# Four one-bank accumulators for the down product, and an earlier request of batch 1's first two row pairs, in a Fourier mix followed by a gated feed-forward network

## The chip, the core and the metric

One core of a Trainium2 chip runs the whole program. The time is device microseconds of one launch; the number that counts is the median of several runs. Inside the profile, times are counted in microseconds from the first instruction of the span. The engines are PE (matrix multiplications, with PEld for its weight loads), DVE, ACT and POOL (elementwise work) and SP, which here only issues DMA transfers.

## The reference

Two stages follow each other. The first is a Fourier mix over 8 sequences (called batches below) of 3008 tokens with 256 features:

```python
X = np.fft.rfft(x, axis=1)
Yr = Xr @ w_r - Xi @ w_i + b_r
Yi = Xr @ w_i + Xi @ w_r + b_i
Yr = np.sign(Yr) * np.maximum(np.abs(Yr) - lam, 0.0)
Yi = np.sign(Yi) * np.maximum(np.abs(Yi) - lam, 0.0)
y = np.fft.irfft(Yr + 1j * Yi, n=x.shape[1], axis=1)
```

The second is a feed-forward network over the 24064 tokens that come out, with 2048 hidden features:

```python
h = x @ w_in
g = h * (1.0 / (1.0 + np.exp(-1.702 * h)))
out = (g @ w_out).astype(np.float32)
```

## The kernel before, in words

**The Fourier part.** `spectral(b, s2)` makes the steps of one batch. Stage A (16 steps, `split_x` and `stage_a`, lines 261 to 288) loads a slice of the input (`xa` or `xr`), multiplies it by a constant matrix (line 283 in plain 32 bits for batches 0 to 2, `mm3` for the others), copies the bank on ACT to `aev` and stores that to a scratch tensor `s1` in DRAM. Stage B (12 steps, `stage_b`) reads back a pair of rows `br` of `s1` with its constants `kr` (`load_b`) and multiplies them (line 312). `load_b(0)` needs all 16 stores of its batch. `stage_b(0)` requests pairs 0 and 1, and each later step requests one pair ahead. `stage_mix` multiplies by the weights, `stage_inv` transforms back and stores `iev` to a scratch tensor `s2`. `tokens` reads `s2` as `ur`, transforms once more (line 408) and splits the tokens of a feed-forward tile into `th` and `tl`.

**The feed-forward part.** Its 47 tiles have 512 tokens each; a tile has eight quarters of the hidden features, q = 0 to 7. `up(q)` makes two banks of 128 by 512 with six matmuls of `mm3` each: a 32-bit product is three products of rounded halves (lines 130, 131 and 132: high by high, high by low, low by high). ACT applies the activation into `gb` (line 440) and rounds it to `hb`; DVE makes the remainder `lb`; sums of them give `gt`, split into `ht` (ACT) and `lt` (DVE), line 127. `down(q)` multiplies them by the weights in the order of the table `ORDER`, seven products of three matmuls of 128 by 256, and adds them up in the accumulator `po` over all eight quarters. The accumulator is one tile of four banks (8 KB in each partition), `self.acc[:, bk, h]`, with one buffer.

**The end of a tile.** After q = 7, `combine` (lines 499 to 511) reads the accumulator: ACT copies bank 0 (line 502), six DVE operations read the banks in the order 1, 2, 3, 1, 1, 2 (lines 503, 504, 505, 506, 508 and 509), POOL adds one pair (line 507), SP stores two outputs. Line 505 is the last reader of bank 3, line 508 that of bank 1, line 509 that of bank 2. The last tile of all has its own `combine_last` (lines 483 to 497), and its last two quarters multiply plain 32-bit values (line 477).

**The order of the work.** A loop over 47 x 8 quarters calls `up(q)`, then `fill(3)`, which takes six entries (three stage A steps) off a list `filler` with stage A of batches 1 and 2, then steps of a queue of later spectral work in proportion to their costs, then `tokens_to`, then `down` of the quarter before. A scheduler reorders each engine's instructions when the program is built: by the dependences between tiles, by a timing model of its own, and by when buffers come free. It follows a tile as a whole: a buffer is free for its next tile when every reader of the old tile is done. The pool `ps_o` holds the accumulator (four banks), the pool `ps_a` four banks `pa` for everything else. Tiles of 128 by 512 (`xr`, `aev`, `br`, `mv`, `yr`, `iev`, `ur`, `o0`, `o1`, `uv` and others) share seven places (`buf2`).

**The start.** `hold_clock` issues a few spare matmuls into a `po` tile while PE would wait.

Of the kernel before, what the change touches and what calls it, by code (L numbers as in the profile page):

```python
# [9 lines left out]
F32 = mybir.dt.float32  # L10
# [5 lines left out]
ALU = mybir.AluOpType  # L16
# [10 lines left out]
TOK, HT = 512, 256  # L27
# [78 lines left out]
def fourier_mix_then_gated_ffn(ctx: ExitStack, tc: tile.TileContext, x, w_r, w_i, b_r, b_i, w_in, w_out, pack, kbs, out):  # L106
    nc = tc.nc
# [6 lines left out]
    ps_o = ctx.enter_context(tc.tile_pool(name="ps_o", bufs=1, space=PSUM))  # L114
    ps_a = ctx.enter_context(tc.tile_pool(name="ps_a", bufs=4, space=PSUM))

    def bank():
        return ps_a.tile([128, 512], F32, name="pa", tag="pa")

    def buf(shape, dt, name, tag=None, bufs=2):  # L120
        return wk.tile(shape, dt, name=name, tag=tag or name, bufs=bufs)

    def buf2(name):
        return buf([128, 2, D], F32, name, tag="w2", bufs=W2)

    def split(hi, lo, src):
        return nc.scalar.copy(hi, src).ins, nc.vector.tensor_tensor(lo, src, hi.bitcast(F32), ALU.subtract).ins  # L127

    def mm3(ps, wh, wl, xh, xl, start=True, stop=True):
        nc.tensor.matmul(ps, lhsT=wh, rhs=xh, start=start, stop=False)  # L130
        nc.tensor.matmul(ps, lhsT=wh, rhs=xl, start=False, stop=False)  # L131
        nc.tensor.matmul(ps, lhsT=wl, rhs=xh, start=False, stop=stop)  # L132
# [38 lines left out]
    wo_h = cst.tile([128, NQ, 7, 128], F32R, name="wo_h")  # L171
    wo_l = cst.tile([128, NQ, 7, 128], F32R, name="wo_l")
# [69 lines left out]
    def spectral(b, s2):  # L242
# [4 lines left out]
        xs, raw, zs, ys = {}, {}, {}, {}  # L247
# [42 lines left out]
        def load_b(sp):  # L290
            if plain:
                kt = buf([128, 3, D], F32, "br0", tag=("zh", "zl")[sp % 2])
                t, k = kt[:, 0:2], kt[:, 2].rearrange("p (i n) -> p i n", i=2)
            else:
                t, k = buf2("br"), buf([128, 2, 2 * N1], F32, "kr")
            with tc.issue_after(stored[13]):
                nc.sync.dma_start(k, kbs[sp])
            nc.sync.dma_start(t, s1r[2 * sp:2 * sp + 2].rearrange("s p d -> p s d"))
            raw[sp] = t, k

        def stage_b(sp):

            ahead = 3 if plain else 1
            for n in range(0 if sp == 0 else sp + ahead, min(sp + ahead + 1, 12)):
                load_b(n)
            t, k = raw.pop(sp)
            co = buf([128, 2, 3, 128], F32, "co")
            pv = bank().rearrange("p (c v i n) -> p c v i n", c=2, v=2, i=2)
            for i in range(2):
                for c in range(2):  # L310
                    cs = slice(128 * c, 128 * c + 128)
                    nc.tensor.matmul(pv[:, c, :, i], lhsT=t[:, i, cs], rhs=k[:, i], start=True, stop=True)  # L312
            nc.scalar.copy(co[:, :, 0:2], pv.rearrange("p c v i n -> p c v (i n)"))
            nc.vector.tensor_tensor(co[:, :, 2], co[:, :, 0], co[:, :, 1], ALU.add)
            z = co.rearrange("p c v n -> p (c v) n")
            if plain:
                zs[sp] = z
                return
            zh = buf([128, 6, 128], F32R, "zh")
            zl = buf([128, 6, 128], F32R, "zl")  # L320
            split(zh, zl, z)
            zs[sp] = zh, zl
# [56 lines left out]
        first, second = [], []  # L379
# [6 lines left out]
            for n in range(4):  # L386
                load_x(n)

        return first, second, preload


    s2s, us, ytiles = {}, {}, {}
# [32 lines left out]
    class Ffn:  # L425
# [43 lines left out]

        def down(self, q):  # L470
            if q == 0:
                self.acc = ps_o.tile([128, 4, 2, HT], F32, name="po", tag="po")
            g = self.g.pop(q)
            for n, (a, t, bk, h) in enumerate(ORDER):
                start, stop = q == 0 and FIRST[bk] == n, q == NQ - 1 and LAST[bk] == n
                if not isinstance(g[t], tuple):
                    nc.tensor.matmul(self.acc[:, bk, h], lhsT=self.w32[q][:, a], rhs=g[t], start=start, stop=stop)
                else:
                    mm3(self.acc[:, bk, h], wo_h[:, q, a], wo_l[:, q, a], *g[t], start=start, stop=stop)
            if q == NQ - 1:  # L480
                (self.combine_last if self.k == NT - 1 else self.combine)()

        def combine_last(self):

            p = self.acc
            o0, o1, uv = buf2("o0"), buf2("o1"), buf2("uv")
            v = nc.vector
            nc.scalar.copy(o0, p[:, 0])
            v.tensor_tensor(uv[:, 0], p[:, 1, 0], o0[:, 0], ALU.add)
            nc.gpsimd.tensor_tensor(o0[:, 0], o0[:, 0], o0[:, 1], ALU.add)  # L490
            v.tensor_tensor(o0[:, 1], uv[:, 0], p[:, 1, 1], ALU.add)
            v.tensor_tensor(uv[:, 1], p[:, 2, 0], uv[:, 0], ALU.add)
            v.tensor_tensor(o0[:, 1], o0[:, 1], p[:, 2, 1], ALU.add)
            nc.sync.dma_start(out[self.k, :, 0], o0.rearrange("p h n -> p (h n)"))
            v.tensor_tensor(o1[:, 1], uv[:, 1], p[:, 1, 1], ALU.add)
            v.tensor_tensor(o1[:, 0], uv[:, 1], p[:, 3, 0], ALU.subtract)
            nc.scalar.dma_start(out[self.k, :, 1], o1.rearrange("p h n -> p (h n)"))

        def combine(self):
            p = self.acc  # L500
            o0, o1, uv = buf2("o0"), buf2("o1"), buf2("uv")
            nc.scalar.copy(o0, p[:, 0])
            nc.vector.tensor_tensor(uv[:, 0], p[:, 1, 0], o0[:, 0], ALU.add)
            nc.vector.tensor_tensor(uv[:, 1], p[:, 2, 0], uv[:, 0], ALU.add)
            nc.vector.tensor_tensor(o1[:, 0], uv[:, 1], p[:, 3, 0], ALU.subtract)
            nc.vector.tensor_tensor(o1[:, 1], uv[:, 1], p[:, 1, 1], ALU.add)
            nc.gpsimd.tensor_tensor(o0[:, 0], o0[:, 0], o0[:, 1], ALU.add)
            nc.vector.tensor_tensor(o0[:, 1], uv[:, 0], p[:, 1, 1], ALU.add)
            nc.vector.tensor_tensor(o0[:, 1], o0[:, 1], p[:, 2, 1], ALU.add)  # L509
            for e, o in enumerate((o0, o1)):  # L510
                nc.sync.dma_start(out[self.k, :, e], o.rearrange("p h n -> p (h n)"))

    def hold_clock(ins, count):

        with tc.issue_after(ins):
            o = ps_o.tile([128, 4, 2, HT], F32, name="po", tag="po").rearrange("p c h n -> p (c h n)")
            for _ in range(count):
                nc.tensor.matmul(o[:96, 0:446], lhsT=ka32, rhs=kc[:96, 0:446], start=True, stop=True)

# [2 lines left out]
    def new_s2(b):  # L522
        s2s[b] = dr.tile([48, 2, NJ, D], F32, name="s2")
        return s2s[b]

    assert NB > 2
    (first, second, _), (first1, queue, preload), (first2, queue2, _) = (spectral(b, new_s2(b)) for b in range(3))
    nextb = 2
    for n, (_, step) in enumerate(first + second):
        step()  # L530
# [8 lines left out]
    filler = first1 + first2  # L539
    last_aev = evacuated[15]  # L540

    def fill(count):
        for _ in range(2 * count):
            if filler:
                filler.pop(0)[1]()

    def weights(q):
        with ExitStack() as held:

            for ins in ([last_aev] if q < 5 else mixed if q == 5 else first_tokens) if q else ():  # L550
                held.enter_context(tc.issue_after(ins))
            up_weights(q, q > 5)
            down_weights(q, q > 5)
# [24 lines left out]
    for n in range(NT * NQ):  # L578
        k, q = divmod(n, NQ)
        if n in (1, 3):  # L580
            weights(6 + n // 2)
        if q == 0:
            cur = Ffn(k)
        cur.up(q)
        fill(3)
        if not queue and nextb < NB:
            if nextb == 2:
                queue = queue2
            else:
                first, second, _ = spectral(nextb, new_s2(nextb))  # L590
                queue = first + [(4000, lambda: None)] + second
            nextb += 1
            total = None
        if queue and total is None and not filler:
            total, spent, n0 = sum(c for c, _ in queue), 0.0, n
            n1 = NQ * S * (nextb - 1) // TOK - 12
        while queue and total and spent < total * (n + 1 - n0) / (n1 - n0):
            c, step = queue.pop(0)
            spent += c
            step()  # L600
        need = TOK * (1 + (n + 2) / NQ)
        while queue and need + JP > S * (nextb - 1):
            queue.pop(0)[1]()
        if JP * done < need:
            tokens_to(need)
        if behind is not None:
            behind[0].down(behind[1])
        behind = (cur, q)
# [37 lines left out]
```

## Time and profile before

| | us |
|---|---|
| median of 3 runs | 2633.46 (2631.92 to 2638.31) |
| the profiled execution | 2632.74 |
| its span, first to last instruction | 2630.6 |
| PE busy in the span | 2589.7 (98%) |
| DVE, ACT, POOL busy | 1967.4, 1642.7, 53.8 |

The page of the profile gives busy times and the clock that PE was granted. The view of waits sums, by pair of instructions, how long an engine stood idle for another. The view by windows gives each engine's busy time and the mean granted clock in stretches of the span. The timeline lists instructions with their start, their length and, in brackets, the idle time before them with what ended it. Matmuls are pipelined, so the distance from one start to the next is what a matmul takes of PE's time; its length is more.

### The profile page before, as it was taken

What the parts mean: (1) busy time and instruction counts of PE and PEld (TensorE: products, weight loads), DVE (VectorE), ACT (ScalarE), POOL (GpSimd) and SP (SyncE); (2) the same over time, 40 slices, a digit from 0 to 9 for tenths busy, and PEclk for the clock granted to TensorE, in tenths of its full rate; (3) what the DMA queues carried; (4) which work ended last, traced back from release to release, by engine and by line L of the source; (5) the groups of instructions that cost most, each with busy time, mean ns of one, the idle gap of its engine ahead of it and who ended that gap; (6) DMA issues with size and microseconds to landing.
All of it is one profiled execution on the core that took longest, in us unless ns stands there. A gap on an engine that the chain in (4) does not pass through costs nothing.

```text
span 2630.6 us, 42804 instructions
## 1 busy us (share of the span) xinstructions
PE 2589.7 (98%) x16520; PEld 2327.6 (88%) x16520; DVE 1967.4 (75%) x3219; ACT 1642.7 (62%) x2547; POOL 53.8 (2%) x71
## 2 busy tenths in 40 slices
PE   7899999999999999999999999999999999999998
PEld 4679999999899998999989999899998999999998
DVE  6767877777777777777777777778777777777676
ACT  5566666666666666666676666766667666655554
POOL 1000000000000000000000000000000000000000
PEclk8899999999999999999999999999999999999999
DMA  8652221111322223212241221322213122200000
GB/s 259 205 171 71 82 86 49 50 59 55 95 79 62 69 62 103 74 60 68 64 124 56 68 67 60 120 63 61 75 60 121 47 74 62 66 18 32 18 20 17
DMA packets 156075, 200.64 MB, mean 76 GB/s; under 512 B 18688, under 2 KB 105600, under 8 KB 155872
## 3 DMA queue, kind: packets, MB, share of 16 engines
q1 hardware_dynamic: 153360, 189.26, 23.7%
q0 software_dynamic: 2368, 8.39, 1.0%
q8 instruction: 130, 2.13, 0.4%
q14 instruction: 73, 0.60, 0.1%
q10 hardware_dynamic: 144, 0.26, 0.0%
HBM read 97.70 MB, written 74.97 MB: 66 GB/s over the span
## 4 chain that ended last, share of the span: by engine, by line
PE 90%; issue 7%; DMA 2%; DVE 1%; ACT 1%; POOL 0%; SPq 0%; POOLq 0%; DVEq 0%; ACTq 0%
PE pa L130 16%; PE pa L131 16%; PE pa L132 16%; PE po L130 11%; PE po L131 11%; PE po L132 11%; PE pa L408 4%; PE pa L312 3%; PE pa L283 1%; PE pa L331 1%; DMA wraw<-in_w_in 1%; DMA s<-aev 0%; PE pa L366 0%; DMA yr<-mv 0%; ACT gb L440 0%
## 5 line engine op out<-in xcount | busy, mean ns | idle before, releaser
L440 ACT ACTIVATE gb<-pa 128x512 f32<-128x512 f32 x752 | 447.0, 598 | 424.0 <-PE pa L132 421.4
L127 DVE TENSOR_TENSOR lt<-gt,ht 128x1024 fp32r<-128x1024 f32 x374 | 458.3, 1226 | 246.8 <-ACT ht L127 245.7
L130 PE MATMUL pa<-th,wi_h 128*128 128x512 f32 x1504 | 597.5, 397 | 2.9 <-ACT gb L440 2.1
L131 PE MATMUL pa<-tl,wi_h 128*128 128x512 f32 x1504 | 591.4, 393 | 0.0
L132 PE MATMUL pa<-th,wi_l 128*128 128x512 f32 x1504 | 588.1, 391 | 0.0
L127 ACT CAST ht<-gt 128x1024 fp32r<-128x1024 f32 x374 | 391.5, 1047 | 158.5 <-DVE gt L462 146.8
L131 PE MATMUL po<-lt,wo_h 128*128 128x256 f32 x1496 | 427.0, 285 | 0.0
L130 PE MATMUL po<-ht,wo_h 128*128 128x256 f32 x1496 | 425.1, 284 | 0.0
L132 PE MATMUL po<-ht,wo_l 128*128 128x256 f32 x1496 | 423.3, 283 | 0.0
L127 DVE TENSOR_TENSOR lb<-gb,hb 128x768 fp32r<-128x768 f32 x375 | 358.7, 957 | 43.2 <-ACT hb L127 41.0
L460 DVE TENSOR_TENSOR gt<-gb 128x512 f32<-128x512 f32 x374 | 261.7, 700 | 134.5 <-ACT gb L440 131.1
L127 ACT CAST hb<-gb 128x768 fp32r<-128x768 f32 x375 | 313.4, 836 | 69.2 <-PE po L132 62.3
L132 PEld LDWEIGHTS pa<-th,wi_l 128*128 128x128 f32 x1504 | 283.5, 188 | 57.3
L130 PEld LDWEIGHTS pa<-th,wi_h 128*128 128x128 f32 x1504 | 284.9, 189 | 52.0 <-ACT gb L440 3.3
L130 PE MATMUL po<-hb,wo_h 128*128 128x256 f32 x1125 | 327.5, 291 | 0.9 <-DVE o L509 0.9
L131 PEld LDWEIGHTS pa<-tl,wi_h 128*128 128x128 f32 x1504 | 284.7, 189 | 44.4 <-DVE wa L198 0.5
L131 PE MATMUL po<-lb,wo_h 128*128 128x256 f32 x1125 | 319.9, 284 | 0.0
L132 PE MATMUL po<-hb,wo_l 128*128 128x256 f32 x1125 | 319.0, 284 | 0.0
L132 PEld LDWEIGHTS po<-ht,wo_l 128*128 128x128 f32 x1496 | 285.7, 191 | 8.6 <-issue 1.7
L131 PEld LDWEIGHTS po<-lt,wo_h 128*128 128x128 f32 x1496 | 285.6, 191 | 8.7 <-issue 1.8
L130 PEld LDWEIGHTS po<-ht,wo_h 128*128 128x128 f32 x1496 | 285.5, 191 | 3.8 <-issue 1.3
L130 PEld LDWEIGHTS po<-hb,wo_h 128*128 128x128 f32 x1125 | 214.8, 191 | 10.1 <-issue 2.6
(123 smaller groups left out, 3780.0 us busy)
## 6 DMA issues: line engine op xcount, KB each, us to landing
s<-aev SPq DMA_DIRECT2D x128, 192.0 KB, 2.6
br<-s SPq DMA_DIRECT2D x96, 256.0 KB, 3.0
yr<-mv SPq DMA_DIRECT2D x384, 64.0 KB, 2.0
s<-iev SPq DMA_DIRECT2D x96, 256.0 KB, 2.3
ur<-s SPq DMA_DIRECT2D x128, 192.0 KB, 2.8
out<-o SPq DMA_DIRECT2D x93, 256.0 KB, 2.1
xr<-in_x SPq DMA_DIRECT2D x80, 192.0 KB, 3.1
kr<-in_kbs SPq DMA_DIRECT2D x84, 128.0 KB, 2.1
```

Of the source, the lines that this page charges most:

```text
L127: return nc.scalar.copy(hi, src).ins, nc.vector.tensor_tensor(lo, src, hi.bitcast(F32), ALU.subtract).ins
L130: nc.tensor.matmul(ps, lhsT=wh, rhs=xh, start=start, stop=False)
L131: nc.tensor.matmul(ps, lhsT=wh, rhs=xl, start=False, stop=False)
L132: nc.tensor.matmul(ps, lhsT=wl, rhs=xh, start=False, stop=stop)
L283: done_a.append(nc.tensor.matmul(ps[:96], lhsT=ka32, rhs=xs.pop(q), start=True, stop=True).ins)
L312: nc.tensor.matmul(pv[:, c, :, i], lhsT=t[:, i, cs], rhs=k[:, i], start=True, stop=True)
L331: nc.tensor.matmul(ps, lhsT=z[:, 3 * c + v], rhs=wf32[v][:, c], start=c == 0, stop=c == 1)
L408: turned.append(nc.tensor.matmul(pv[:, c, 94 * j:94 * j + 94], lhsT=t[:, j, 128 * c:128 * c + 128], rhs=kz, start=True, stop=True).ins)
L440: nc.scalar.activation(o, ps.rearrange("p (h n) -> p h n", h=2), AF.Gelu_apprx_sigmoid)
L460: nc.vector.tensor_tensor(gt[:, 0:2], b12, gb[:, 0:3:2], ALU.subtract)
```

## The change

It has two parts.

The accumulator becomes four tiles of one bank, each with a name and a buffer of its own (`po0` to `po3`). The matmuls and the operations of `combine` and `combine_last` are the same and read the same data. What differs is what the scheduler may assume: each bank is free for the next tile when its own last reader is done, a reader of one bank waits for the matmuls into that bank, and matmuls into different banks are not tied to each other.

The rows of batch 1's pairs 0 and 1 are requested by a new `preload_b`, which the loop calls once after `fill(3)` when at most 12 entries of `filler` are left. These 12 are six stage A steps of batch 2; batch 1's stage A has been issued in full by then. `stage_b` leaves out requests that were made.

```diff
             for n in range(0 if sp == 0 else sp + ahead, min(sp + ahead + 1, 12)):
-                load_b(n)
+                if n not in raw:
+                    load_b(n)
...
-        return first, second, preload
+        def preload_b():
+            load_b(0)
+            load_b(1)
+
+        return first, second, preload, preload_b
...
             if q == 0:
-                self.acc = ps_o.tile([128, 4, 2, HT], F32, name="po", tag="po")
+                self.acc = [ps_o.tile([128, 2, HT], F32, name="po", tag=f"po{i}") for i in range(4)]
...
-                    mm3(self.acc[:, bk, h], wo_h[:, q, a], wo_l[:, q, a], *g[t], start=start, stop=stop)
+                    mm3(self.acc[bk][:, h], wo_h[:, q, a], wo_l[:, q, a], *g[t], start=start, stop=stop)
...
-            nc.scalar.copy(o0, p[:, 0])
-            nc.vector.tensor_tensor(uv[:, 0], p[:, 1, 0], o0[:, 0], ALU.add)
+            nc.scalar.copy(o0, p[0])
+            nc.vector.tensor_tensor(uv[:, 0], p[1][:, 0], o0[:, 0], ALU.add)
...
-            o = ps_o.tile([128, 4, 2, HT], F32, name="po", tag="po").rearrange("p c h n -> p (c h n)")
+            o = ps_o.tile([128, 2, HT], F32, name="po", tag="po0").rearrange("p h n -> p (h n)")
...
         cur.up(q)
         fill(3)
+        if preload_b and len(filler) <= 12:
+            preload_b()
+            preload_b = None
```

The built programs have the same number of instructions on PE, DVE, ACT, POOL and SP. Their order differs from about the first quarter of tile 0 on. Three places matter below. Line numbers of the changed kernel are up to eight higher than before.

SP, at the end of stage A of batch 2, before the change (`s1_87` is that batch's scratch tensor, `s1_85` that of batch 1, `aev` the stored slices, `xa` the loaded ones):

```order
L288 DMA s1_87<-aev_1537 96x512
L288 DMA s1_87<-aev_1544 96x512
L259 DMA xa_1604<-in_x 96x512
L288 DMA s1_87<-aev_1601 96x512
L288 DMA s1_87<-aev_1608 96x512
L288 DMA s1_87<-aev_1613 96x512
L288 DMA s1_87<-aev_1668 96x512
L298 DMA br_1676<-s1_85 128x2x256
L298 DMA br_1680<-s1_85 128x2x256
L288 DMA s1_87<-aev_1673 96x512
```

And with it:

```order
L288 DMA s1_87<-aev_1540 96x512
L288 DMA s1_87<-aev_1547 96x512
L298 DMA br_1550<-s1_85 128x2x256
L298 DMA br_1554<-s1_85 128x2x256
L259 DMA xa_1615<-in_x 96x512
L288 DMA s1_87<-aev_1612 96x512
L288 DMA s1_87<-aev_1619 96x512
L288 DMA s1_87<-aev_1624 96x512
L288 DMA s1_87<-aev_1679 96x512
```

The two requests of `br` stand six stores earlier, between the last two loads of `xa`.

PE, at the start of stage A of batch 4, which falls together with the end of a feed-forward tile, before the change (`pa_10737` is the second bank of an `up`, `pa_10769` that of the first stage A step):

```order
L131 MATMUL po_10182<-lt_10597,wo_h_80 128x256
L132 MATMUL po_10182<-ht_10596,wo_l_81 128x256
L131 MATMUL pa_10737<-tl_9884,wi_h_78 128x512
L132 MATMUL pa_10737<-th_9883,wi_l_79 128x512
L130 MATMUL pa_10737<-th_9883,wi_h_78 128x512
L131 MATMUL pa_10737<-tl_9884,wi_h_78 128x512
L132 MATMUL pa_10737<-th_9883,wi_l_79 128x512
L130 MATMUL pa_10769<-xh_10765,ka_73 96x512
L130 MATMUL pa_10782<-xh_10778,ka_73 96x512
L408 MATMUL pa_10791<-kc_69,ur_10542 128x94 x4
```

And with it (`po_10846` to `po_10849` are the four banks of the next tile):

```order
L132 MATMUL po_10847<-ht_10720,wo_l_81 128x256
L130 MATMUL po_10846<-hb_10793,wo_h_80 128x256
L130 MATMUL po_10848<-hb_10717,wo_h_80 128x256
L131 MATMUL po_10848<-lb_10718,wo_h_80 128x256
L132 MATMUL po_10848<-hb_10717,wo_l_81 128x256
L130 MATMUL po_10848<-ht_10720,wo_h_80 128x256
L131 MATMUL po_10848<-lt_10721,wo_h_80 128x256
L132 MATMUL po_10848<-ht_10720,wo_l_81 128x256
L130 MATMUL po_10848<-hb_10793,wo_h_80 128x256
L130 MATMUL pa_10817<-xh_10813,ka_73 96x512
L130 MATMUL pa_10830<-xh_10826,ka_73 96x512
```

The first matmul on `xh` stood directly behind the six matmuls of an `up`; now the last `up` before it ends 23 matmuls earlier, all 23 of the next tile's `down`.

PE, at the end of the program, before the change (`po_27752` is the accumulator, L477 the plain 32-bit products):

```order
L131 MATMUL po_27752<-lb_27992,wo_h_80 128x256
L132 MATMUL po_27752<-hb_27991,wo_l_81 128x256
L130 MATMUL po_27752<-hb_27991,wo_h_80 128x256
L131 MATMUL po_27752<-lb_27992,wo_h_80 128x256
L132 MATMUL po_27752<-hb_27991,wo_l_81 128x256
L477 MATMUL po_27752<-gl_27993,w32_27994 128x256 x4
L477 MATMUL po_27752<-gb_28022,w32_28040 128x256 x3
L477 MATMUL po_27752<-gl_28039,w32_28040 128x256 x4
```

And with it (`po_27890` is bank 0, then 27891, 27892 and 27893 are banks 1, 2 and 3; their plain products are on L482):

```order
L130 MATMUL po_27892<-hb_28132,wo_h_80 128x256
L131 MATMUL po_27892<-lb_28133,wo_h_80 128x256
L132 MATMUL po_27892<-hb_28132,wo_l_81 128x256
L482 MATMUL po_27891<-gl_28134,w32_28135 128x256
L482 MATMUL po_27892<-gl_28134,w32_28135 128x256
L482 MATMUL po_27892<-gb_28163,w32_28181 128x256
L482 MATMUL po_27891<-gl_28134,w32_28135 128x256
L482 MATMUL po_27891<-gl_28180,w32_28181 128x256 x2
L482 MATMUL po_27893<-gl_28134,w32_28135 128x256
L482 MATMUL po_27892<-gl_28180,w32_28181 128x256
L482 MATMUL po_27893<-gl_28180,w32_28181 128x256
```

Bank 0 has no matmul among these last ones any more, bank 1 ends three matmuls and bank 2 one matmul ahead of the last. DVE's last six operations were lines 489, 491, 492, 493, 495 and 496 in this order; in the changed program, in the numbers of before, they are 489 (bank 1), 492 (bank 2), 491 (bank 1), 495 (bank 1), 496 (bank 3) and 493 (bank 2).

More of the change, by code (lines that the diff above doesn't have):

```diff
@@ L476, in down @@
                 if not isinstance(g[t], tuple):
-                    nc.tensor.matmul(self.acc[:, bk, h], lhsT=self.w32[q][:, a], rhs=g[t], start=start, stop=stop)
+                    nc.tensor.matmul(self.acc[bk][:, h], lhsT=self.w32[q][:, a], rhs=g[t], start=start, stop=stop)
                 else:
-                    mm3(self.acc[:, bk, h], wo_h[:, q, a], wo_l[:, q, a], *g[t], start=start, stop=stop)
+                    mm3(self.acc[bk][:, h], wo_h[:, q, a], wo_l[:, q, a], *g[t], start=start, stop=stop)
             if q == NQ - 1:
@@ L487, in combine_last @@
             v = nc.vector
-            nc.scalar.copy(o0, p[:, 0])
-            v.tensor_tensor(uv[:, 0], p[:, 1, 0], o0[:, 0], ALU.add)
+            nc.scalar.copy(o0, p[0])
+            v.tensor_tensor(uv[:, 0], p[1][:, 0], o0[:, 0], ALU.add)
             nc.gpsimd.tensor_tensor(o0[:, 0], o0[:, 0], o0[:, 1], ALU.add)
-            v.tensor_tensor(o0[:, 1], uv[:, 0], p[:, 1, 1], ALU.add)
-            v.tensor_tensor(uv[:, 1], p[:, 2, 0], uv[:, 0], ALU.add)
-            v.tensor_tensor(o0[:, 1], o0[:, 1], p[:, 2, 1], ALU.add)
+            v.tensor_tensor(o0[:, 1], uv[:, 0], p[1][:, 1], ALU.add)
+            v.tensor_tensor(uv[:, 1], p[2][:, 0], uv[:, 0], ALU.add)
+            v.tensor_tensor(o0[:, 1], o0[:, 1], p[2][:, 1], ALU.add)
             nc.sync.dma_start(out[self.k, :, 0], o0.rearrange("p h n -> p (h n)"))
-            v.tensor_tensor(o1[:, 1], uv[:, 1], p[:, 1, 1], ALU.add)
-            v.tensor_tensor(o1[:, 0], uv[:, 1], p[:, 3, 0], ALU.subtract)
+            v.tensor_tensor(o1[:, 1], uv[:, 1], p[1][:, 1], ALU.add)
+            v.tensor_tensor(o1[:, 0], uv[:, 1], p[3][:, 0], ALU.subtract)
             nc.scalar.dma_start(out[self.k, :, 1], o1.rearrange("p h n -> p (h n)"))
@@ L501, in combine @@
             o0, o1, uv = buf2("o0"), buf2("o1"), buf2("uv")
-            nc.scalar.copy(o0, p[:, 0])
-            nc.vector.tensor_tensor(uv[:, 0], p[:, 1, 0], o0[:, 0], ALU.add)
-            nc.vector.tensor_tensor(uv[:, 1], p[:, 2, 0], uv[:, 0], ALU.add)
-            nc.vector.tensor_tensor(o1[:, 0], uv[:, 1], p[:, 3, 0], ALU.subtract)
-            nc.vector.tensor_tensor(o1[:, 1], uv[:, 1], p[:, 1, 1], ALU.add)
+            nc.scalar.copy(o0, p[0])
+            nc.vector.tensor_tensor(uv[:, 0], p[1][:, 0], o0[:, 0], ALU.add)
+            nc.vector.tensor_tensor(uv[:, 1], p[2][:, 0], uv[:, 0], ALU.add)
+            nc.vector.tensor_tensor(o1[:, 0], uv[:, 1], p[3][:, 0], ALU.subtract)
+            nc.vector.tensor_tensor(o1[:, 1], uv[:, 1], p[1][:, 1], ALU.add)
             nc.gpsimd.tensor_tensor(o0[:, 0], o0[:, 0], o0[:, 1], ALU.add)
-            nc.vector.tensor_tensor(o0[:, 1], uv[:, 0], p[:, 1, 1], ALU.add)
-            nc.vector.tensor_tensor(o0[:, 1], o0[:, 1], p[:, 2, 1], ALU.add)
+            nc.vector.tensor_tensor(o0[:, 1], uv[:, 0], p[1][:, 1], ALU.add)
+            nc.vector.tensor_tensor(o0[:, 1], o0[:, 1], p[2][:, 1], ALU.add)
             for e, o in enumerate((o0, o1)):
@@ L526, in fourier_mix_then_gated_ffn @@
     assert NB > 2
-    (first, second, _), (first1, queue, preload), (first2, queue2, _) = (spectral(b, new_s2(b)) for b in range(3))
+    (first, second, *_), (first1, queue, preload, preload_b), (first2, queue2, *_) = (spectral(b, new_s2(b)) for b in range(3))
     nextb = 2
@@ L589, in fourier_mix_then_gated_ffn @@
             else:
-                first, second, _ = spectral(nextb, new_s2(nextb))
+                first, second, *_ = spectral(nextb, new_s2(nextb))
                 queue = first + [(4000, lambda: None)] + second
```

## The prediction

> **What bounds the kernel now.** I read the page first, then PE's waits, then the windows around them.
>
> ```profile
> span 2630.6 us, 42804 instructions
> ...
> PE 2589.7 (98%) x16520; PEld 2327.6 (88%) x16520; DVE 1967.4 (75%) x3219; ACT 1642.7 (62%) x2547; POOL 53.8 (2%) x71
> ...
> PEclk8899999999999999999999999999999999999999
> ```
>
> PE is busy for 98% of the span, and the change leaves its matmuls as they are. So it can win only what PE loses: the 41 us in which it is idle, and stretches at a lower clock. The waits of PE that the change can reach, in the view of waits (total, times, longest), are these.
>
> ```profile
> PE pa L312 <- DMA br<-s: 2.2, 1, 2.2
> PE pa L130 <- ACT xh L127: 2.1, 1, 2.1
> PE pa L130 <- ACT gb L440: 2.1, 3, 0.7
> PE po L130 <- DVE o L509: 0.9, 1, 0.9
> PE pa L130 <- DVE mv L336: 0.9, 2, 0.5
> ```
>
> The wait that the four banks should remove, the next tile's first down matmul on line 509, costs PE 0.9 us, once in 46 tile ends. The windows place all the losses (PE's busy time comes first behind the length).
>
> ```profile
> 193.00:205.00 12.00, 9.81 (x55) 8.78 (x54) 7.49 (x14) 6.65 (x11) 0.72 (x1) 0.86 0.56 181
> 205.00:1010.00 805.00, 804.58 (x5321) 737.48 (x5321) 615.72 (x998) 512.10 (x788) 12.76 (x14) 1.00 0.22 67
> 1010.00:1025.00 15.00, 12.89 (x68) 10.75 (x67) 11.91 (x20) 9.55 (x15) 0.73 (x1) 0.89 0.35 106
> 1025.00:2600.00 1575.00, 1571.51 (x10223) 1430.89 (x10222) 1184.45 (x1896) 990.53 (x1520) 25.53 (x30) 1.00 0.21 64
> 2600.00:2631.00 31.00, 23.67 (x149) 21.31 (x147) 16.51 (x28) 9.18 (x13) 0.72 (x1) 0.96 0.05 17
> ```
>
> Between 205 and 2600 us PE idles 0.4 + 2.1 + 3.5 = 6.0 us in 2395. At 193 to 205 it idles 2.2 us, and in the last window 7.3 us. The earlier idle time lies ahead of the first instruction that the change moves on PE (at about 131 us), so I leave it.
>
> **The change part by part.** *The request of br.* PE and then SP, around the start of batch 1's stage B:
>
> ```profile
> 194.76 0.28 PE L132 MATMUL po<-ht,wo_l 128*128 128x256 f32 x1
> 197.23 2.86 PE L312 MATMUL pa<-kr,br 128*128 128x128 f32 x16 [2.19 <-DMA br<-s]
> ```
> ```profile
> 185.69 8.01 SPq L288 DMA_DIRECT2D s<-aev  x4
> 193.79 0.92 SPq L298 DMA_DIRECT2D br<-s  x2
> ```
>
> The two requests (line 298) stood behind four stores of batch 2, the last of which SP could issue only at about 193.7; the rows landed at 197.1, 3.3 us after the request. Now they stand ahead of these four stores, so they go out before 185.7 and land by 189, some 4 us ahead of need. The 2.19 us of idle PE go. The clock goes with them:
>
> ```profile
> 199.00:200.00 1.00, 1.00 (x7) 1.00 (x6) 1.00 (x3) 0.00 (x0) 0.70 (x1) 0.50 0.49 158
> ```
>
> About 1 us behind the gap the granted clock is at 0.50. The window of 12 us has a mean of 0.86, so 12 x 0.14 = 1.7 us of PE's time are lost on top, and the term is 2.2 + 1.7 = 3.9 us. [...]
>
> What the move costs: each br takes one of seven places that the next aev copies want, and SP waits at it for the landing of an earlier store, with the last load of xa and four stores queued behind. That load is made three stage A steps ahead of its use, and these steps lie about 2 us apart there (four stores, one a step, over 8.0 us in the row above), so a wait of some 2 to 3 us, like the 3.3 us that br's rows took to land, is covered by 6; without the cover they would fall on PE. I take nothing, with 3 us as the other end.
>
> *The tail.* PE's last matmuls, and all that follows them:
>
> ```profile
> 2621.78 1.89 PE L477 MATMUL po<-gl,w 128*128 128x256 f32 x8
> 2623.71 0.59 ACT L488 COPY o<-po 128x512 f32<-128x512 f32 x1 [6.55 <-PE po L477]
> 2624.33 0.43 DVE L489 TENSOR_TENSOR uv<-po,o 128x256 f32<-128x256 f32 x1 [5.52 <-ACT o L488]
> 2624.83 0.72 POOL L490 TENSOR_TENSOR o<-o 128x256 f32<-128x256 f32 x1 [35.13 <-DVE uv L489]
> 2625.59 0.42 DVE L491 TENSOR_TENSOR o<-uv,po 128x256 f32<-128x256 f32 x1 [0.83 <-POOL o L490]
> 2625.93 0.42 DVE L492 TENSOR_TENSOR uv<-po,uv 128x256 f32<-128x256 f32 x1
> 2626.92 0.41 DVE L496 TENSOR_TENSOR o<-uv,po 128x256 f32<-128x256 f32 x1
> ```
>
> ACT's copy of bank 0 waits for the very last matmul, which writes bank 3. From PE's end (2623.67) to DVE's (2627.33) it takes 3.66 us, and 3.3 us more for the last store. Now the copy, line 489 and POOL's sum run while PE still works: bank 1 ends three matmuls early, at 1.89 / 4 = 0.47 us each. Line 492 can start 0.47 us before PE's end, when bank 2 is complete. Four operations follow at 0.33 us from start to start (2625.59 to 2625.93), the last ending 0.41 us after its start: -0.47 + 0.04 + 4 x 0.33 + 0.41 = 1.3 us behind PE's end. The gain is 3.66 - 1.3 = 2.4 us at most. Against it, the order of the tail's matmuls is new: the last quarter's plain products of bank 0 now wait for the last activation with some two dozen short matmuls between, where before all other down products stood there. The bound from the other side is nothing gained; I take 1.9 us.
>
> *The new order of matmuls.* With four tiles the scheduler mixes `up` and `down` more finely; by my count of the two programs PE changes from 256-wide to 512-wide matmuls 702 times, before 575 times. The first fence has the last 256-wide matmul of a run and the start of a run of 512-wide ones, the second a pair far inside one:
>
> ```profile
> 1012.66 0.28 PE L132 MATMUL po<-hb,wo_l 128*128 128x256 f32 x1
> 1012.78 0.40 PE L130 MATMUL pa<-th,wi_h 128*128 128x512 f32 x1
> 1013.02 0.40 PE L131 MATMUL pa<-tl,wi_h 128*128 128x512 f32 x1
> ```
> ```profile
> 2608.35 0.39 PE L132 MATMUL pa<-th,wi_l 128*128 128x512 f32 x1
> 2608.57 0.39 PE L130 MATMUL pa<-th,wi_h 128*128 128x512 f32 x1
> ```
>
> From start to start the 256-wide one takes 0.12 us, the 512-wide one behind it 0.24, and the one of the second fence 0.22. So 127 more entries cost up to 127 x 0.02 = 2.5 us, or nothing if the entries are short runs; I take 1.0.
>
> *The waits in between.* The largest, at the start of batch 4 (PE, then ACT):
>
> ```profile
> 1019.22 1.00 PE L130 MATMUL pa<-xh,ka 96*96 96x512 f32 x2 [2.07 <-ACT xh L127]
> ```
> ```profile
> 1017.19 0.60 ACT L440 ACTIVATE gb<-pa 128x512 f32<-128x512 f32 x1 [0.58 <-PE pa L132]
> 1017.82 0.83 ACT L127 CAST hb<-gb 128x768 fp32r<-128x768 f32 x1
> 1018.56 0.61 ACT L127 CAST xh<-xr 96x512 fp32r<-96x512 f32 x1
> ```
>
> ACT does the activation of the `up` that PE has just ended, then hb, then xh, and PE has nothing else in its order. It idles 2.1 us, and the window's clock of 0.89 over 15 us adds 1.7: 3.8 us. In the changed order 23 matmuls of `down` stand between that `up` and xh. At 0.12 us each they last 2.8 us, more than the 2.1 that PE idles. This gap should go. It is an accident of the order, though, and a new order has accidents of its own. The other 3.9 us I leave as large as they are.
>
> What is new in kind lies at the 46 tile ends. The next tile's down matmuls may now be placed nearer to `combine`, bank by bank. The one place where they wait today (PE, then DVE):
>
> ```profile
> 2055.15 0.36 PE L130 MATMUL po<-hb,wo_h 128*128 128x256 f32 x1 [0.92 <-DVE o L509]
> ```
> ```profile
> 2053.27 0.41 DVE L505 TENSOR_TENSOR o<-uv,po 128x256 f32<-128x256 f32 x1
> 2054.60 0.41 DVE L509 TENSOR_TENSOR o<-o,po 128x256 f32<-128x256 f32 x1
> ```
>
> Bank 3 is free at line 505's end, 1.3 us before line 509 frees bank 2, so this wait shrinks or goes. But two such waits of 0.75 us elsewhere cost the 1.5 us that I put against the gap at 1017: net 3.8 - 1.5 = 2.3 us gained, with bounds from 7.7 gained (6.0 idle and 1.7 of clock all gone) to 4 lost (another gap like the one at 1017 and none removed).
>
> *The sum* against the profiled execution's 2632.74 us: - 3.9 - 1.9 + 1.0 - 2.3 = - 7.1, which gives 2625.6. The median of the runs before is 0.7 above that execution, so 2633.46 - 7.1 = 2626.4.
>
> **The rivals.** *The gaps only move (nothing net in the middle).* The new order has as many accidents as the old. Then - 3.9 - 1.9 + 1.0 = - 4.8 and 2628.7; if a gap takes the place of the one at 195 too, because L312 then waits for something else, 2632. For it: three of the five waits above are of kinds that neither part touches.
>
> *The order closes nearly all gaps.* With banks free one by one PE always finds down work: - 3.9 - 2.4 - 7.7 + 0.5 = - 13.5, or 2620.0. For it: PE idles so seldom that one good order is enough. Against: the scheduler's model sets that order, not the chip.
>
> *The tile ends begin to wait: slower.* The first matmul into each bank stands closer to the release, and DVE's queue holds other work between the lines of `combine` (line 462's sum stood between 508 and 509 at 2054 us). A mean wait of 0.35 us at 46 ends is 16 us, or five gaps like that at 1017 (3.8 us with their clock) are 19. With the 5.8 us of the first two terms gained, it decides from a mean of 0.13 us at 46 ends on, and at 0.35 us it gives 2633.46 - 5.8 + 1.0 + 16 = 2644.7. Against: of 46 ends today one waits. [...]
>
> *The request is not early.* If SP held at the br rows until the aev store has landed and stage A slipped by it, the gap at 195 would turn into one at 190: 2633.46 - 1.9 + 1.0 - 2.3 = 2630.3.
>
> **How the numbers follow.** About 0.3%, or 7.9 us, is what a measurement of this kernel can tell from no change; faster means below 2625.6, slower above 2641.4. My forecast has 0.48, spread from 2623 to 2630 by the tail (0 to 2.4) and the accidents, with a third of it under 2625.6. Gaps only moved, or an ineffective request: 0.24 together. All gaps closed: 0.22. Tile ends that wait: 0.06, nearly all of it slower. So faster 0.16 + 0.22 = 0.38, slower 0.05, the same 0.57. The range for 8 in 10 reaches from 2620 (gaps closed) to 2632 (gaps moved) and leaves out the slower case.
>
> **What would show it right or wrong.** Right: no wait of L312 (L313 in the changed file) on br near 195, and no half clock there; from PE's last matmul to DVE's last operation 1.3 us and not 3.7; no gap of 2 us at batch 4's start; idle PE between 205 and 2600 of about 4 us. Wrong: a new gap of 2 us or more with half clock behind it, waits of po matmuls on lines 505 to 509 at many tile ends, or a PE span that grows while its idle time does not.

## The result and the profile after

The changed kernel takes 2620.14 us in the median of 6 runs (2619.57 to 2622.23), before 2633.59 us (2631.92 to 2638.31, 6 runs). The ratio is 0.9947 with a 95% interval of 0.9934 to 0.9960: faster, by 13.5 us. I forecast 7.1 us as the likeliest gain and put the chance of a gain above 0.3% at 0.38; the time came out at the value of the rival in which the order closes nearly all gaps (2620.0). By its terms that is partly chance, as shown further down.

The page of the changed kernel, with the three ACT groups used further down (busy time, then mean length in ns):

```profile
span 2617.8 us, 42900 instructions
...
PE 2584.1 (99%) x16520; PEld 2323.9 (89%) x16520; DVE 1965.8 (75%) x3219; ACT 1644.3 (63%) x2547; POOL 57.4 (2%) x71
...
L445 ACT ACTIVATE gb<-pa 128x512 f32<-128x512 f32 x752 | 448.0, 597 | 457.4 <-PE pa L132 454.9
...
L127 ACT CAST ht<-gt 128x1024 fp32r<-128x1024 f32 x374 | 391.6, 1047 | 149.7 <-DVE gt L467 144.6
...
L127 ACT CAST hb<-gb 128x768 fp32r<-128x768 f32 x375 | 313.6, 836 | 33.3 <-PE po L132 25.9
```

The 96 more instructions than before are semaphore operations, by balance; the engines' work is the same in number. PE's idle time in the span fell from 2630.6 - 2589.7 = 40.9 us to 33.7. The view of waits between 190 and 2605 us, where five pairs stood before, has one left:

```profile
PE po L131 <- DVE lb L127: 1.6, 1, 1.6
```

The windows at the places of the prediction (length, then PE's busy time; the mean granted clock stands behind the five engines):

```profile
193.00:205.00 12.00, 12.00 (x88) 10.98 (x87) 10.41 (x20) 7.74 (x13) 0.73 (x1) 1.00 0.42 137
205.00:1010.00 805.00, 805.00 (x5321) 738.44 (x5320) 615.43 (x999) 513.64 (x791) 15.39 (x14) 1.00 0.22 68
1010.00:1025.00 15.00, 15.00 (x95) 13.28 (x94) 12.26 (x22) 9.91 (x17) 0.74 (x1) 1.00 0.51 155
1025.00:2600.00 1575.00, 1573.30 (x10242) 1433.66 (x10241) 1189.39 (x1900) 996.15 (x1522) 26.50 (x30) 1.00 0.21 64
```

Between 205 and 2600 us PE idles 1.7 us where it idled 6.0, and both windows with half clock, 0.86 and 0.89 before, show 1.00.

SP at the end of batch 2's stage A:

```profile
182.02 1.00 SPq L298 DMA_DIRECT2D br<-s  x2
186.40 0.34 SPq L259 DMA_DIRECT2D xa<-in_x  x1
```

The two requests leave at 182.0 us in place of 193.8, and the load of `xa` behind them follows at 186.4 (185.1 before) without a wait of PE.

The tail, PE's last matmuls and then DVE:

```profile
2609.97 2.75 PE L482 MATMUL po<-gl,w 128*128 128x256 f32 x12
```
```profile
2611.53 0.42 DVE L494 TENSOR_TENSOR uv<-po,o 128x256 f32<-128x256 f32 x1 [3.75 <-issue]
2612.33 0.42 DVE L497 TENSOR_TENSOR uv<-po,uv 128x256 f32<-128x256 f32 x1 [0.38 <-PE po L482]
2612.79 0.42 DVE L496 TENSOR_TENSOR o<-uv,po 128x256 f32<-128x256 f32 x1
2613.13 0.41 DVE L500 TENSOR_TENSOR o<-uv,po 128x256 f32<-128x256 f32 x1
2613.46 0.41 DVE L501 TENSOR_TENSOR o<-uv,po 128x256 f32<-128x256 f32 x1
2613.79 0.41 DVE L498 TENSOR_TENSOR o<-o,po 128x256 f32<-128x256 f32 x1
```

PE ends at 2612.72. Line 494 (489 before) runs 1.2 us ahead of that, line 497 (492) 0.4 us ahead, and four operations follow: DVE ends 1.5 us behind PE, before 3.7.

**What I had not looked at: where in a tile the waits lie.** Here is the place of the longest one in the kernel before once more, this time with what stands around it: the last down product of a tile on PE, the copy of bank 0, line 509, and the next tile's first down product.

```profile
1015.70 0.28 PE L132 MATMUL po<-ht,wo_l 128*128 128x256 f32 x1
...
1016.02 0.59 ACT L502 COPY o<-po 128x512 f32<-128x512 f32 x1 [0.94 <-PE po L132]
...
1020.37 0.41 DVE L509 TENSOR_TENSOR o<-o,po 128x256 f32<-128x256 f32 x1
...
1023.63 0.41 PE L130 MATMUL po<-hb,wo_h 128*128 128x256 f32 x1
```

For 7.9 us PE has no down product. Until 1020.78, the end of line 509, it can have none, because the one tile of four banks cannot be written again before; the order then puts the first one 2.9 us later still. The gap at 1017 lies inside. So do all the others: I took the 46 stretches between the last down matmul of a tile and the first of the next, from start to start. The first runs from 194.76 to 205.06 us and holds the wait on br; the other 45 are 431 of the 2395 us from 205 to 2600 (18%) and hold all 6.02 us of PE's idle time there. The same place in the changed kernel:

```profile
1008.92 0.59 ACT L507 COPY o<-po 128x512 f32<-128x512 f32 x1
...
1011.03 0.28 PE L132 MATMUL po<-ht,wo_l 128*128 128x256 f32 x1
...
1012.77 0.28 PE L130 MATMUL po<-hb,wo_h 128*128 128x256 f32 x1
...
1013.35 0.41 DVE L513 TENSOR_TENSOR o<-uv,po 128x256 f32<-128x256 f32 x1
```

Both ends have moved. ACT's copy of bank 0 starts 2.1 us before the tile's last down matmul, since bank 0 is complete earlier; and the next tile's down products begin while `combine` still has sums to do. The stretch without down products is 1.7 us long in place of 7.9.

### The profile page after: what moved, and what is told of

Read it like the earlier page. It is cut to its first block, busy times and chain, and to the rows that moved or that the text cites. A ratio compares the mean times of both kernels' runs of the same rounds, so it can differ in the third digit from the quotient of the medians.

```text
span 2617.8 us, 42900 instructions
## 1 busy us (share of the span) xinstructions
PE 2584.1 (99%) x16520; PEld 2323.9 (89%) x16520; DVE 1965.8 (75%) x3219; ACT 1644.3 (63%) x2547; POOL 57.4 (2%) x71
## 4 chain that ended last, share of the span: by engine, by line
PE 95%; DMA 2%; issue 2%; DVE 0%; ACT 0%; SPq 0%; POOL 0%; POOLq 0%; DVEq 0%; ACTq 0%
PE pa L130 17%; PE pa L131 17%; PE pa L132 17%; PE po L130 12%; PE po L131 12%; PE po L132 12%; PE pa L413 4%; PE pa L313 3%; PE pa L332 1%; PE pa L283 1%; DMA wraw<-in_w_in 1%; DMA wraw<-in_w_out 0%; DMA s<-aev 0%; DMA xa<-in_x 0%; DMA br<-s 0%
## 5 line engine op out<-in xcount | busy, mean ns | idle before, releaser
L131 PE MATMUL po<-lt,wo_h 128*128 128x256 f32 x1496 | 408.7, 286 | 0.0
L132 PE MATMUL po<-ht,wo_l 128*128 128x256 f32 x1496 | 405.3, 284 | 0.0
L127 DVE TENSOR_TENSOR lb<-gb,hb 128x768 fp32r<-128x768 f32 x375 | 360.3, 961 | 26.9 <-ACT hb L127 25.7
L130 PE MATMUL po<-ht,wo_h 128*128 128x256 f32 x1496 | 354.6, 284 | 0.1
L130 PE MATMUL po<-hb,wo_h 128*128 128x256 f32 x1125 | 320.6, 294 | 0.0
L130 PEld LDWEIGHTS po<-ht,wo_h 128*128 128x128 f32 x1496 | 259.0, 190 | 10.3 <-issue 1.8
L131 PEld LDWEIGHTS po<-lb,wo_h 128*128 128x128 f32 x1125 | 214.4, 191 | 10.8 <-DVE lb L127 1.8
```

## The experiments

Two theories stood against each other for the 4.3 us of waits that went between 205 and 2600 us. Theory 1: they are a property of the one tile, which keeps PE from any down product at each tile end. Theory 2: the order is a draw, as the prediction had it ("a new order has accidents of its own"), and this one was lucky. For each kernel I worked out from its order how much PE time stands between the down products of one tile and the next (0.12 us for a 256-wide matmul, 0.227 for a 512-wide one; 46 ends). All ratios are to the kernel before on the same chip. The labels are explained run by run below.

| kernel | order: us without down products | PE idle, 210 to 2600 us | ratio (95%) |
|---|---|---|---|
| before | 394 | 6.0 | 1 |
| early rows only | 398 | 6.3 | 0.9982 (0.9973 to 0.9991) |
| before, shifted 14 | 400 | 4.7 | 0.9981 (0.9972 to 0.9990) |
| before, shifted 11 | 401 | 6.0 | 0.9987 (0.9978 to 0.9995) |
| four tiles held as one | 390 | 6.9 | 0.9974 (0.9962 to 0.9985) |
| banks released together | 353 | 2.5 | 0.9944 (0.9930 to 0.9957) |
| two tiles 0+1, 2+3 | 310 | 2.6 | 0.9950 (0.9937 to 0.9964) |
| two tiles 0+3, 1+2 | 302 | 6.3 | 0.9979 (0.9970 to 0.9988) |
| copies held | 202 | 2.1 | 0.9950 (0.9937 to 0.9962) |
| changed | 153 | 1.7 | 0.9947 (0.9934 to 0.9960) |
| last copy held | 153 | 1.7 | 0.9949 (0.9937 to 0.9962) |
| four banks only | 152 | 1.6 | 0.9953 (0.9940 to 0.9965) |
| changed, shifted 14 | 148 | 0.8 | 0.9938 (0.9925 to 0.9950) |
| changed, shifted 13 | 145 | 0.6 | 0.9941 (0.9928 to 0.9953) |

**Four banks only.** The changed kernel without the early request:

```diff
-        if preload_b and len(filler) <= 12:
-            preload_b()
-            preload_b = None
```

> The accumulator as four tiles alone; br's rows are requested where they were. Theory 1 (release at the tile ends: every PE wait of the kernel before between 205 and 2600 us lies between the last down product of a tile and the first of the next, because one tile of four banks comes free only at line 509): by its order PE has 152 us of other work in these stretches in place of 394, so the waits between 205 and 2600 us fall from 6 us to 2 or less, the half clock at 1021 us goes, the tail is 1.9 us shorter, and the wait on br with its half clock (2.2 + 1.7 us) stays: 2633.6 - 13.5 + 3.9 = 2624.0 us. Theory 2 (the order is a draw, and the changed kernel drew well): the waits are of another number and at other places, also outside the tile ends; 4 to 8 us of them, some 2628 us.

Measured: 2623.60 us. PE's waits from 190 to 2605 us:

```profile
PE po L131 <- DVE lb L127: 1.6, 1, 1.6
PE pa L313 <- DMA br<-s: 1.5, 1, 1.5
```

The waits of the middle are gone without the early rows, and the wait on br stays (1.5 us in place of 2.2, and this time without a half clock: the mean is 1.00 from 190 to 210 us, before 0.91). Theory 1's waits, 2 us or less, are met (1.6). That the time is met too (2624.0 forecast) is luck in part: the wait on br cost 1.5 us and not 3.9, and behind the wait on lb this run has a half clock at 2044 us, worth 1.7 us, that the changed kernel has not. From 220 us on PE's order is that of the changed kernel, so this is no second draw of four tiles.

**Early rows only.** The diff's lines on `load_b` and `preload_b`, put into the kernel before; `po` stays one tile.

```diff
         fill(3)
+        if preload_b and len(filler) <= 12:
+            preload_b()
+            preload_b = None
```

> The rows of br requested sooner alone; one accumulator tile of four banks. Both theories: no wait of PE on br near 195 us and no half clock behind it, 3.9 us. Theory 1: the waits at the tile ends remain in size, 5 to 8 us with their clock, all within the tile ends: 2629.7 us. Theory 2: they fall anywhere and are drawn anew, 2 to 8 us: 2626 to 2631 us.

Measured: 2629.98 us, against 2629.7. The waits:

```profile
PE pa L130 <- ACT xh L127: 2.1, 1, 2.1
PE pa L130 <- ACT gb L445: 2.1, 3, 0.7
PE po L130 <- DVE o L514: 1.1, 1, 1.1
PE pa L130 <- DVE mv L337: 0.9, 2, 0.5
```

The wait on br is gone, and the four others of the kernel before are all back, 6.26 us of idle time, all of it inside the tile ends. PE's order between 205 and 2600 us differs from that before at only 438 of some 15,600 places, and the gaps are the same ones, so this run does not test theory 2.

**Last copy held.** In `combine_last` of the changed kernel the copy waits for the tile's last matmul (`self.end`); `behind_of` makes its first instruction wait for its second:

```diff
-            nc.scalar.copy(o0, p[0])
+            behind_of(nc.scalar.copy(o0, p[0]).ins, self.end)
```

> The changed kernel, but ACT's copy of bank 0 in the last tile waits for the very last matmul, as it does in the kernel before. If the tail's 1.9 us come from this copy's early start, the time from PE's end to DVE's last operation goes from 1.5 back to about 3.7 us and the kernel takes 2620.1 + 2.0 = 2622.1 us. If they come from the new order of the tail's matmuls, it stays at 2620.1.

Measured: 2621.50 us. PE's order is that of the changed kernel to the last matmul; ACT copies at 2612.00, behind PE's end at 2611.96, and DVE's last operation is this one:

```profile
2614.66 0.41 DVE L501 TENSOR_TENSOR o<-o,po 128x256 f32<-128x256 f32 x1
```

It ends 3.1 us behind PE, 1.6 us later than in the changed kernel. Of the 2.2 us that the tail gained at this point the copy's early start is 1.6. The time itself cannot tell this apart from the changed kernel (0.9949 and 0.9947).

**Banks released together.** Four tiles, but the first matmul into each bank waits for the last sum of the tile before (`combine` notes it in `released`):

```diff
+                    if start and released:
+                        behind_of(one, released[-1])
```

> The changed kernel with four tiles, but the first matmul of the next tile into each bank waits for the last sum of combine, so that all four banks come free together, as the one tile did; the copy of bank 0 still starts early. Theory 1: PE has 353 us of other work in the stretches without down products, near the 394 of before, so waits of 4 to 6 us come back there, with a half clock if one of them is about 2 us long: 2624 to 2628 us. Theory 2, or if the gain lies in the finer mixing alone: no more waits than in the changed kernel, 2620 to 2621 us.

Measured: 2619.93 us. The waits:

```profile
PE po L130 <- DVE o L522: 2.5, 2, 1.9
```

The new wait is there, on combine's last sum, but only 2.5 us of it and none on gb or mv. As I had put it, with the release alone as the cause, theory 1 missed: 2624 to 2628 us was expected. What this kernel leaves free is the tile's other end, the copy of bank 0 that starts before the last down matmul.

**Four tiles held as one.** So both ends were held: the edit above, and in `combine` the copy behind the tile's last matmul. **Copies held** has the second edit alone.

```diff
-            nc.scalar.copy(o0, p[0])
+            behind_of(nc.scalar.copy(o0, p[0]).ins, self.end)
```

> Four tiles that behave as the one did at every tile end but the last: the copy of bank 0 waits for the tile's last down matmul, and the next tile's first matmul into each bank waits for combine's last sum. By its order PE has 390 us without down products at the tile ends (394 before, 353 with only the release held, 153 in the changed kernel). Theory 1, now with both halves (late start of combine and joint release): PE's waits between 205 and 2600 us come back to about 6 us, with some on ACT's gb and on mv, and 2624 to 2626 us with a half clock behind a 2 us wait. Theory 2 (the order is a draw): as with the release alone held, 1.5 to 3 us of waits, 2620 to 2621 us.

> The changed kernel, but in each tile except the last the copy of bank 0 waits for the tile's last down matmul; the banks come free one by one. By its order 202 us without down products at the tile ends. Theory 1: these stretches stay short (4.1 us in the median), so PE's waits stay at 2 us or less and the time at 2620 to 2621 us. Theory 2: waits of another number, 1 to 6 us, 2619 to 2626 us.

Measured: 2628.62 us with both held. The waits:

```profile
PE po L130 <- DVE o L521: 3.9, 2, 2.3
PE pa L130 <- ACT gb L450: 2.1, 3, 0.7
PE pa L130 <- DVE mv L337: 1.0, 2, 0.5
```

This is the kernel before again, with four tiles: three waits on gb of 2.1 us together, two on mv, one of 2.3 us at batch 4's start, and a half clock behind that (from 1018 us on). The rise over 2620.1 is 8.5 us, more than the 4 to 6 expected: 5.2 us of idle time and 1.7 of clock account for 6.9, and up to 190 us, ahead of the first tile end, this profiled run idles 3 us more than the changed one. With the copies alone held it is 2621.77 us and 2.1 us of waits, both a little above the 2620 to 2621 us and the 2 us expected, with a half clock at 2043:

```profile
PE po L131 <- DVE lb L127: 1.3, 1, 1.3
PE po L130 <- ACT o L510: 0.7, 1, 0.7
```

So neither end alone makes the waits; the tile as the unit of both does.

**Shifted.** For other orders, one number of the schedule is changed in both kernels, by which batch's work is spread over the tiles:

```diff
-            n1 = NQ * S * (nextb - 1) // TOK - 12
+            n1 = NQ * S * (nextb - 1) // TOK - 14
```

> The kernel before with one number of the schedule changed (stage work of a batch is spread so that it ends 14 quarters ahead, in place of 12), which gives another order of all its matmuls; 400 us without down products at the tile ends. Theory 1: 5 to 8 us of waits between 205 and 2600 us, all within tile ends, 2631 to 2637 us. Theory 2: a new draw, 1 to 8 us of waits, 2626 to 2636 us.

> The changed kernel with the same number changed; 148 us without down products at the tile ends. Theory 1: 2 us of waits between 205 and 2600 us or less, 2619 to 2621 us. Theory 2: a new draw, 1 to 8 us, 2619 to 2627 us.

> The kernel before with that number at 11, a third order of one tile; 401 us without down products at the tile ends. Theory 1: 4 to 8 us of waits between 205 and 2600 us, all within tile ends, 2629 to 2637 us. Theory 2: 1 to 8 us, anywhere, 2626 to 2636 us.

> The changed kernel with the stage work of a batch ending 13 quarters ahead in place of 12, a third order of four tiles; 145 us without down products at the tile ends. Theory 1: 2 us of waits between 205 and 2600 us or less, 2617 to 2621 us. Theory 2: 1 to 8 us, 2618 to 2627 us.

Measured: 2629.59 and 2631.87 us for the one tile, 2618.17 and 2618.79 us for four. The waits of the kernel before at 14, and of the changed kernel at 14:

```profile
PE po L130 <- DVE o L509: 3.6, 6, 1.5
PE pa L312 <- DMA br<-s: 2.9, 1, 2.9
PE pa L130 <- DVE mv L336: 1.1, 2, 0.6
```
```profile
PE po L130 <- ACT hb L127: 0.8, 1, 0.8
```

The waits of the one tile are others now (six on line 509, none on gb), so the order is a new one, yet there are 4.7 us of them (a little below the 5 to 8 expected, as the time is below its 2631 to 2637), all within the tile ends; at 11 it is 6.0 us, of which 0.1 lies outside. Four tiles have 0.8 and 0.6 us, less than theory 2's 1 to 8, and at 14 the time is a little below theory 1's 2619 to 2621. In all three orders of four tiles (changed, 14, 13) none of PE's idle time from 205 to 2600 us lies within a tile end any more. Where a wait falls and what it is on is a draw; how much of it there is in all is not: with one tile, or four held as one, 4.7 to 6.9 us, with four tiles whose banks come free one by one 0.6 to 2.1. Each run of one tile by itself would fit theory 2's wide ranges; that the two groups do not overlap, and that the four held as one give the old waits back, does not fit it. On three orders to a side, theory 2 falls.

**Two tiles.** The changed kernel with two tiles of two banks:

```diff
-                self.acc = [ps_o.tile([128, 2, HT], F32, name="po", tag=f"po{i}") for i in range(4)]
+                two = [ps_o.tile([128, 2, 2, HT], F32, name="po", tag=f"po{i}") for i in range(2)]
+                self.acc = [two[0][:, 0], two[1][:, 0], two[1][:, 1], two[0][:, 1]]
```

> The changed kernel with the accumulator as two tiles of two banks, 0 with 3 and 1 with 2. By its order PE has 302 us without down products at the tile ends (394 before, 390 with four tiles held as one, 153 changed). Theory 1: PE's waits between 205 and 2600 us lie between: 2 to 4 us, nearer to the changed kernel's 1.7 than to 6, since waits on ACT's gb need a stretch that fills four pa banks; in the last tile the copy waits for bank 3's last matmul again, so the tail is long again: 2621 to 2625 us. Theory 2: any number of waits.

> The same with 0 and 1 in one tile, 2 and 3 in the other; 310 us without down products at the tile ends. Theory 1: as for the other pairing, 2 to 4 us of waits between 205 and 2600 us, 2621 to 2625 us. Theory 2: any number of waits.

Measured: 2628.41 us for 0 with 3, 2621.57 us for 0 with 1. The second is as expected (2.6 us of waits); the first is not. The waits of the first, then of the second:

```profile
PE po L130 <- DVE o L511: 5.8, 3, 3.9
PE pa L130 <- ACT gb L445: 0.5, 2, 0.3
```
```profile
PE po L130 <- DVE o L514: 2.6, 2, 1.7
```

One wait of 3.9 us in the first, at 2041 us, makes most of it, and 6.8 us of half clock follow (256-wide matmuls start 0.21 us apart from 2045.7 us on, 0.12 ahead of the wait). There the next tile's first down matmul stands directly behind the old tile's last in PE's order, so it is the order that trusted the release and the chip that was late: DVE did lines 465 and 466 and a remainder `lb` between its sums. That is the rival of the waiting tile ends, at three of 46. Nearly the same length without down products (302 and 310 us) goes with 6.3 and 2.6 us of waits, so this length does not set the size of the loss by itself; what else does for two tiles, these runs leave open.

None of the runs is clearly ahead of the changed kernel: its shifted forms, at 0.9938 and 0.9941, lie within its interval.

## Why the prediction was right or wrong

**br.** Right. 3.9 us were forecast; the window from 193 to 205 us went from 9.81 us busy at a clock of 0.86 to 12.00 at 1.00, that is 2.2 + 1.7 us, and the early rows alone gave 0.18% (0.09 to 0.27), 2.4 to 7.1 us. No wait on SP fell on PE. But the 1.7 us are no fixed price of such a gap: with four banks only, PE waited 1.5 us here, at 11 2.1 us, both at full clock (1.00 from 190 to 210 us).

**The tail.** Right. 1.9 us were taken; from PE's end to the end of the span it is 2617.8 - 2612.7 = 5.1 us, before 2630.6 - 2623.7 = 6.9, so 1.8 to 1.9. DVE ends 1.5 us behind PE, where 1.3 was worked out.

**The finer mixing.** 1.0 us of loss was taken; none shows. PE's busy time is 5.6 us smaller, and the half-clock stretches that went (at 99, 198 and 1021 us, 3.41 us each, half of which is lost) account for 5.1. The mixing is not what won the time either: with the banks released together PE goes from 256-wide to 512-wide matmuls 594 times by the prediction's count, near the 575 of before, and the time is that of the changed kernel.

**The waits in between.** Here the prediction failed, and with it the forecast of no measurable change. 2.3 us were forecast: the gap at 1017 (3.8 us) against 1.5 of new ones, "an accident of the order, though, and a new order has accidents of its own. The other 3.9 us I leave as large as they are." It was 4.3 us of idle time and the 1.7 of clock, 6.0 us. The gap at 1017 went as forecast, and the new waits came to 1.6 us (one, on lb) where 1.5 were put down; that match is luck, because they were priced as waits on a release and this one is not. The step that failed is the 3.9 us "as large as they are": beside the wait on lb PE idles only 0.1 us in the changed kernel. Behind it was the reading of the waits by the names in the view: br, xh, gb, o, mv, of which "three of the five waits above are of kinds that neither part touches". The name is what PE waited for last. What the waits have in common is that for some 9 us at each tile end only `up` and spectral work were left to PE, and the runs with the ends held show that they come and go with this. Why that work does not always keep PE busy is open. An `up` takes PE 12 matmuls of 0.23 us from start to start, 2.8 us, and ACT, by the rows of the page, two activations, hb and ht, 2 x 0.597 + 0.836 + 1.047 = 3.1 us, which would make ACT the slower of the two. But ACT is not full there: over the 46 stretches in the kernel before it is busy 294.9 of 441.3 us (67%; 63% from 205 to 2600 us). DVE, which does the sums of `combine` in them, is nearer to it with 383.8 us (87%; 76% from 205 to 2600). The view that would have told it is the timeline around each of the seven gaps over 0.15 us: the last `po` before it and the first behind it.

**The sum.** In the trace 3.9 + 1.9 + 6.0 = 11.8 us of the 12.8 by which the span fell. The rest lies up to 190 us, where PE idles 1.2 us more and the half clock at 99 us (1.7 us) is gone, and in what single matmuls vary. The profiled runs of the other kernels idle 25.7 to 29.9 us up to 190, so about 1 us either way there says nothing of the change.

**The rivals.** That all gaps close was given 0.22. "Against: the scheduler's model sets that order, not the chip": that objection counted for too much: the change removes a tie that no order could get around. The rival's 2620.0 was met, but not its terms: it had 7.7 us in the middle and 2.4 at the tail where the trace has 6.0 and 1.9, and about 1 us of the gain is in none of the three. The slower one, tile ends that wait for a bank, did not happen with the four tiles of the changed kernel, whose granted clock is 1.00 from 210 to 2600 us; with two tiles of 0 with 3 it did, at three tile ends. (The mean wait from which it was to decide, 0.13 us, leaves out the 1.0 us of mixing that its 2644.7 has in it; with that it is 4.8 / 46 = 0.10.)

## What to carry to other kernels

When an engine is busy for 98%, find out for each of its few gaps what is missing from its queue there, not only what it waited for last; if every gap lies in the same phase of the loop, suspect one cause, and test it by putting back what was taken away. An accumulator of several banks that is one tile to the scheduler holds up work at both ends, the first reader until the last bank is written and the first writer until the last bank is read; one tile to a bank cuts both, and holding either end alone gave back at most 0.8 of the 4.3 us. A mechanism that was priced for one place should be searched for at all others before the rest is called chance.

## What the runs showed of the hardware

The stretches at half clock did not begin a fixed time behind a gap: in the kernel before one began 1.0 us behind the end of the wait on br (197.23 us, then 198.21), the next 1.6 us behind that of the wait on xh (1019.22, then 1020.82). In the profiles of the kernels before and changed their begins lie on a grid of 3.413 us from the first of them on, which is also the length of the three at 99, 198 and 1021 us (198.21 and 1020.82 are 241.0 cells apart). The length of a wait does not say by itself whether a stretch follows. With four banks only and with the changed kernel, the same wait on lb, 1.62 us long, fell differently on the grid; cells of the first, then of the second (PE's busy time first behind the length, the clock behind the five engines):

```profile
2041.06:2044.47 3.41, 1.79 (x13) 1.48 (x13) 3.41 (x6) 0.80 (x1) 1.64 (x1) 1.00 0.00 0
2044.47:2047.88 3.41, 3.41 (x17) 3.17 (x16) 1.99 (x6) 0.28 (x1) 0.00 (x0) 0.50 0.50 147
```
```profile
2037.66:2041.07 3.41, 2.09 (x17) 1.79 (x15) 2.70 (x4) 1.62 (x3) 1.64 (x1) 1.00 0.00 0
2041.07:2044.48 3.41, 3.03 (x25) 2.83 (x25) 2.85 (x9) 0.62 (x2) 0.00 (x0) 1.00 0.31 93
```

All 1.62 us in one cell, 47% of it: the next cell ran at 0.50. Split into 1.32 and 0.30: it ran at 1.00. The cells of the two waits of the kernel before, from 194.79 and from 1017.41 us, were idle for 64 and 54%, and the next ran at 0.50; with the banks released together the cell from 1013.10 us was idle for 49% (1.73 of 3.41 us busy), and the next ran at 1.00. So the idle share of a cell does not settle it either: 47% went with half clock and 49% with full clock, and what else counts was not shown. A wait of about 2 us had no one price in these runs: the 2.1 us on br at shift 11 cost 2.1 us, with the clock at 1.00 from 190 to 210 us; the 2.2 us on br before cost 3.9, 1.7 of it by the clock.
